# The first tile's maxima and subtractions head by head, and the matrix of one from a count by GpSimd

## The chip, the cores and the metric

The kernel runs on one core of one Trainium2 chip. The metric is the device time of one execution in microseconds: 1178.03 us is the median of 3 runs of the kernel before (1176.53 to 1178.63). The engines are named as in the profile: PE (TensorE), DVE (VectorE), ACT (ScalarE), POOL (GpSimd) and SP (SyncE, which here only issues DMAs).

## The reference

Block-causal attention, whose output goes straight through a gated feed-forward layer. Inputs: q, k, v of 8 batches x 8 heads x 576 positions x 64; weights 512 x 1536 (two) and 1536 x 512.

```python
scores = q @ k.transpose(0, 1, 3, 2) / sqrt(64)
scores = where(pos_i // 64 >= pos_j // 64, scores, -1e9)   # blocks of 64
scores = scores - scores.max(-1)
attn = exp(scores); attn = attn / (attn.sum(-1) + 1e-9)
x = (attn @ v).transpose(0, 2, 1, 3).reshape(4608, 512)
g = x @ w_gate
out = (g / (1 + exp(-g)) * (x @ w_val)) @ w_out
```

## The kernel before

The 4608 rows of x are cut into 18 tiles of 256. Attention works on pairs of heads. Scores stand transposed, keys on the 128 partitions and queries along a row, so that the maximum over keys is taken first over chunks of 128 keys (DVE) and then over the partitions (POOL, a partition all-reduce, L709). The feed-forward of a tile starts when the four head pairs of its rows are done; the first tile needs only queries and keys 0 to 255 of batch 0, and that piece of attention runs first of all.

In the code the function `attention` lists this work as tasks, each with an engine, a cost, a rank and the tasks it waits for. A planner (`in_order`) plays the costs through and writes one list of tasks per engine; the program runs those lists as they stand. Each engine is in order, so an instruction that waits holds all behind it. SP's and ACT's lists also hold the DMA issues: a DMA that waits for a landing or a semaphore holds the later ones of its queue.

For the first tile (`whole` in the code, `stays` set) the scores of a head pair are not copied out of PSUM. One PSUM buffer (`at` or `po`) has two banks, one for each head; a bank holds 384 scores per partition: 256 queries against keys 0 to 127 (chunk 0) and queries 128 to 255 against keys 128 to 255 (chunk 1). For a head pair the steps are:

- SP and ACT load q and k (L387), PE turns them with the help of the matrix of one `ident` (L411), ACT copies them out (L419), PE multiplies (L437).
- ACT hides, in place, the first 64 queries of each chunk from the upper 64 keys (L479), both heads and both chunks in one instruction; ACT copies chunk 0's queries 128 to 255 of both heads to `mx` (L482).
- DVE copies chunk 0's queries 0 to 127 of both heads to `mx` (L702) and takes the maximum of `mx` and chunk 1 (L705).
- POOL reduces `mx` over the partitions, one instruction per head (L709).
- DVE subtracts `mx` from both chunks, both heads at a time, from PSUM into `sc` (L733); ACT takes exp (L737); PE multiplies with v and with ones (L777); DVE divides (L804 to L811).

Before all that, at the program's start, DVE fills `ident`: a memset and seven doublings give the column number (L308, L311), a transposition and three additions the row number (L312, L315), and a comparison the matrix (L316). POOL at the same time zeroes two buffers for v (L260), two for `ob` (L281) and two tails of `parts` (L234). The first load of v (L754) is the third DMA of SP's list and waits for the first of these memsets.

Of the kernel before, what the change touches and what calls it, by code (L numbers as in the profile page):

```python
# [9 lines left out]
I32 = mybir.dt.int32  # L10
# [8 lines left out]
def kernel(  # L19
# [96 lines left out]
    def tiles_of(tag, place, variant=""):  # L116
        pool, variants = kinds[tag]
        slot = slots[tag][place]
        if slot[0] != variant:
            shapes, init = variants[variant]  # L120
            names = [f"{tag}{place}_{k}" for k in range(len(shapes))]
            slot[:] = variant, [
                x and pool.tile(*x, name=name, tag=name, bufs=1) for x, name in zip(shapes, names)
            ]
            if init:
                init(*slot[1])
        return slot[1]
# [36 lines left out]
    def act_us(n, psum=False, more=0.0):  # L164
        return (0.05 if psum else 0.093) + n * 0.000833 + more

    def dve_us(n, one=False):
        return 0.07 + n * (0.00052 if one else 0.00104)
# [128 lines left out]
    pool_of(psum, "gv", 2, [([P, 2 * XT], F32)])  # L297
    pool_of(psum, "po", 1, [([P, 2, DM], F32)])

    first_of = [("v", ""), ("ob", "signs" if wide else "out"), ("parts", "pair"), ("xhl", ""), ("wo", "raw"), ("hhl", "")]  # L300
    for tag, variant in first_of:
        for place in range(len(slots[tag])):
            tiles_of(tag, place, variant)


    scratch = tiles_of("t", 0)[0]
    count, mine = scratch[:, 0:P], scratch[:, P : P + 32]
    nc.vector.memset(count[:, 0:1], 0.0)  # L308
    for i in range(7):
        n = 2**i  # L310
        nc.vector.tensor_scalar(count[:, n : 2 * n], count[:, 0:n], float(n), None, ALU.add)  # L311
    nc.vector.transpose(mine, count[:, 0:32])  # L312
    for i in range(1, P // 32):
        rows = slice(32 * i, 32 * (i + 1))
        nc.vector.tensor_scalar(mine[rows, 0:1], mine[rows, 0:1], 32.0 * i, None, ALU.add)  # L315
    nc.vector.tensor_scalar(ident, count, mine[:, 0:1], None, ALU.is_equal)  # L316

    x_d = dram.tile([DM, NT], F32, name="x_d")
    s_d = dram.tile([H, NT], F32, name="s_d")
# [22 lines left out]
    def attention(R, b, h, a, e, early, bufs, lane):  # L342
# [31 lines left out]
        def piece(c, lo=0):  # L374
            return sc[0][:, :, place[c] + lo : place[c] + e - first[c]]


        def plain_scores():
# [49 lines left out]
            for visit in visits:  # L428
# [19 lines left out]
                for parts, ps in zip(visit, both):  # L448
# [25 lines left out]
                    if whole:  # L474
                        stays.append(ps)

                        def hide_there(ps=ps):
                            x = ps[0].rearrange("p x (n w) -> p x n w", w=2 * P)[:, :, :, 0:BLK]
                            nc.scalar.activation(x, x, AF.Identity, bias=unseen)  # L479

                        def max_there(ps=ps):
                            nc.scalar.copy(mx[0][:, :, L + P : L + W], ps[0][:, :, P:W])  # L482

                        t = add("ACT", act_us(4 * BLK) + 0.1, Q, hide_there, [pr], [ps])
                        t = add("ACT", act_us(2 * W), Q, max_there, [t], [ps, mx])
                        evac[0].append(t)
                        evac[1].append(t)
                        continue
# [208 lines left out]
            return stays[0][0][:, :, o + lo : o + e - first[c]]  # L697

        def merged(c, into, op, of=piece):
            if stays and op == ALU.max:  # L700

                nc.vector.tensor_copy(into[0][:, :, L : L + P], of(0)[:, :, 0:P])  # L702
            into = into[0][:, :, L + first[c] - a : L + W]
            prev = of(0, first[1] - a) if c == 1 and not stays else into
            nc.vector.tensor_tensor(into, prev, of(c), op)  # L705

        def max_all(x):
            m = mx[0][:, x, L : L + W]
            nc.gpsimd.partition_all_reduce(m, m, channels=P, reduce_op=bass_isa.ReduceOp.max)  # L709

        later = [c for run in runs for c in run if c > 1]
        ms = []
        for c in (1, *later):
            ms.append(
                add(
                    "DVE",
                    dve_us(2 * (e - first[c])),
                    Q,
                    lambda c=c: merged(c, mx, ALU.max, scores_of),
                    [*evac[0], *evac[c], *ms[0:1], *ms[-1:]],  # L720
                    [*stays, sc, mx],
                    not stays,
                )
            )
# [3 lines left out]
        exps, taken = {}, []  # L728
        for run in runs:

            def minus(c):
                m = mx[0][:, :, L + first[c] - a : L + W]
                nc.vector.tensor_tensor(piece(c), scores_of(c), m, ALU.subtract)  # L733

            def exponent(run=run):
                x = sc[0][:, :, place[run[0]] : place[run[-1]] + e - first[run[-1]]]
                nc.scalar.activation(x, x, AF.Exp)  # L737

            subs = [
                add("DVE", dve_us(2 * (e - first[c])), R, lambda c=c: minus(c), mm, [*stays, sc, mx], not stays)  # L740
                for c in run
            ]
            t = add("ACT", act_us(2 * sum(e - first[c] for c in run)), R, exponent, subs, [sc])
            exps.update({c: t for c in run})
            taken += subs
# [668 lines left out]
```

## Time and profile before

| what | value |
|---|---|
| median of 3 runs | 1178.03 us (1176.53 to 1178.63) |
| profiled execution: time, span | 1175.4 us, 1173.6 us |
| mean granted TensorE clock | 0.996 |
| PE busy | 1145.5 us, 98% of the span |
| DVE, ACT, POOL busy | 758.9, 620.4, 325.5 us |
| DMA moved | 197.40 MB, mean 168 GB/s |

A busy share is a mean over stages with different limits. In the 40 slices of the page (29.3 us each) PE shows 5, 8, 8 and then 9 to the end but for the last slice, which shows 8: PE stands idle in the first 88 us almost alone, and the changed lines all lie in the first 31 us. The views of that stretch are what matters here.

### The profile page before, as it was taken

Reading aid. Unit: us, or ns where it says so; the run is one execution under the profiler, and the core shown is the slowest. Engines: PE = TensorE matmul, PEld = TensorE weight load, DVE = VectorE, ACT = ScalarE, POOL = GpSimd, SP = SyncE. Lnnn points to the kernel's source line nnn. Section 1 sums busy time; section 2 is a strip of 40 time slices with the busy share of each in tenths; the row PEclk is TensorE's granted clock in tenths of the full one; section 3 lists DMA queues with packets and bytes.
Section 4 is the critical chain, followed back from the end, with each engine's and each line's share of the span. In section 5 each row is a group of like instructions: output and inputs, shape, how many; then the busy total and the mean of one; then the engine's idle time right before and its main releaser. Section 6 shows DMA issues by size and latency. Waiting matters only on the chain.

```text
span 1173.6 us, 21780 instructions
## 1 busy us (share of the span) xinstructions
PE 1145.5 (98%) x8512; PEld 1024.7 (87%) x8512; DVE 758.9 (65%) x1230; ACT 620.4 (53%) x1114; POOL 325.5 (28%) x139
## 2 busy tenths in 40 slices
PE   5889999999999999999999999999999999999998
PEld 4568778898898989988998899898989899999997
DVE  6988988575887668768575859575767533323222
ACT  6978876546573837465656555555646312212111
POOL 3222100144535251434444334252432500000000
PEclk9989999999999999999999999999999999999999
DMA  8658756766564756656565565655663445444432
GB/s 225 188 151 219 201 187 226 206 178 166 169 148 137 198 164 167 195 166 168 152 188 160 152 177 163 187 146 161 164 202 108 145 148 197 140 167 136 143 134 100
DMA packets 266982, 197.40 MB, mean 168 GB/s; under 512 B 195264, under 2 KB 231376, under 8 KB 266880
## 3 DMA queue, kind: packets, MB, share of 16 engines
q1 hardware_dynamic: 264304, 195.29, 56.9%
q8 instruction: 67, 1.10, 0.4%
q10 hardware_dynamic: 2576, 0.72, 0.3%
q14 instruction: 35, 0.29, 0.1%
HBM read 171.57 MB, written 24.38 MB: 167 GB/s over the span
## 4 chain that ended last, share of the span: by engine, by line
PE 85%; DVE 5%; ACT 4%; DMA 3%; issue 1%; POOL 1%; SPq 1%; ACTq 0%; DVEq 0%; POOLq 0%
PE gv L1100 16%; PE gv L1102 15%; PE gv L1101 15%; PE po L1191 7%; PE po L1193 7%; PE po L1192 7%; PE at L777 7%; PE at L564 6%; DVE sc L733 1%; DVE mx L705 1%; DMA wo<-in_moe_w_val_dram 1%; POOL mx L709 1%; DMA wo<-in_moe_w_out_dram 1%; ACT ob L959 1%; PE at L648 1%
## 5 line engine op out<-in xcount | busy, mean ns | idle before, releaser
L709 POOL PARTITION_ALL_REDUCE mx<-mx x80 | 144.1, 1850 | 408.7 <-issue 135.2
L1100 PE MATMUL gv<-xhl,v_all 128*128 128x256 f32 x864 | 241.8, 280 | 0.8 <-DVE t L1136 0.7
L1102 PE MATMUL gv<-xhl,v_all 128*128 128x256 f32 x864 | 239.7, 277 | 0.0
L1101 PE MATMUL gv<-xhl,v_all 128*128 128x256 f32 x864 | 239.3, 277 | 0.0
L828 POOL PARTITION_ALL_REDUCE mx<-mx x48 | 178.9, 3775 | 201.4 <-DVE mx L705 192.8
L1136 DVE SCALAR_TENSOR_TENSOR t<-t,gv 128x512 f32<-128x512 f32 x108 | 74.0, 685 | 215.4 <-ACT t L1133 215.2
L1100 PEld LDWEIGHTS gv<-xhl,v_all 128*128 128x128 f32 x864 | 162.1, 188 | 4.9 <-issue 2.5
L1101 PEld LDWEIGHTS gv<-xhl,v_all 128*128 128x128 f32 x864 | 162.3, 188 | 0.6
L1102 PEld LDWEIGHTS gv<-xhl,v_all 128*128 128x128 f32 x864 | 162.2, 188 | 0.2
L1133 ACT ACTIVATE t<-gv 128x512 f32<-128x512 f32 x108 | 64.6, 598 | 171.2 <-PE gv L1102 171.1
L1191 PE MATMUL po<-wo,hhl 128*128 128x512 f32 x372 | 147.7, 397 | 0.0
L1192 PE MATMUL po<-wo,hhl 128*128 128x512 f32 x372 | 145.6, 391 | 0.0
L1193 PE MATMUL po<-wo,hhl 128*128 128x512 f32 x372 | 145.1, 390 | 0.2 <-DVE hhl L1149 0.2
L1146 ACT CAST hhl<-t 128x512 fp32r<-128x512 f32 x108 | 67.0, 620 | 132.1 <-DVE t L1141 129.7
L733 DVE TENSOR_TENSOR sc<-sc,mx 128x640 f32<-128x640 f32 (+6 forms) x168 | 122.7, 765 | 11.7 <-POOL mx L709 11.6
L737 ACT ACTIVATE sc<-sc 128x1024 f32<-128x1024 f32 (+3 forms) x104 | 106.0, 1029 | 45.3 <-DVE sc L733 44.9
L1100 PE MATMUL gv<-xhl,g_even 128*128 128x256 f32 x432 | 123.7, 286 | 0.0
L1102 PE MATMUL gv<-xhl,g_even 128*128 128x256 f32 x432 | 122.2, 283 | 0.4 <-DVE g_even L981 0.4
L1101 PE MATMUL gv<-xhl,g_even 128*128 128x256 f32 x432 | 122.1, 283 | 0.0
L1100 PE MATMUL gv<-xhl,g_odd 128*128 128x256 f32 x432 | 120.7, 279 | 0.0
L1101 PE MATMUL gv<-xhl,g_odd 128*128 128x256 f32 x432 | 119.6, 277 | 0.0
L1102 PE MATMUL gv<-xhl,g_odd 128*128 128x256 f32 x432 | 119.6, 277 | 0.0
(171 smaller groups left out, 2368.8 us busy)
## 6 DMA issues: line engine op xcount, KB each, us to landing
wo<-wo_d SPq DMA_DIRECT2D x200, 512.0 KB
out_dram<-ob SPq DMA_DIRECT2D x35, 256.0 KB
v<-in_v_dram SPq DMA_DIRECT2D x64, 128.0 KB
xt<-x_d SPq DMA_DIRECT2D x64, 128.0 KB
rt<-r_d SPq DMA_DIRECT2D x128, 64.0 KB
qk<-in_q_dram SPq DMA_DIRECT2D x112, 72.0 KB
qk<-in_k_dram SPq DMA_DIRECT2D x104, 72.0 KB
x_d<-xu SPq DMA_DIRECT2D x24, 288.0 KB
```

The costliest lines, as they stand in the source:

```text
L709: nc.gpsimd.partition_all_reduce(m, m, channels=P, reduce_op=bass_isa.ReduceOp.max)
L733: nc.vector.tensor_tensor(piece(c), scores_of(c), m, ALU.subtract)
L737: nc.scalar.activation(x, x, AF.Exp)
L777: nc.tensor.matmul(ps[0][own(x), 1 - i if sums else i, q0 - s0 : s1 - s0], lhsT=ones if sums else vt[0][:, 2 * lane + c, own(x)], rhs=sc[0 ...
L828: nc.gpsimd.partition_all_reduce(m, m, channels=P, reduce_op=bass_isa.ReduceOp.add)
L1100: nc.tensor.matmul(o, lhsT=hi[:, d], rhs=xhi[:, 0:w], start=first, stop=False)
L1101: nc.tensor.matmul(o, lhsT=hi[:, d], rhs=xlo[:, 0:w], start=False, stop=False)
L1102: nc.tensor.matmul(o, lhsT=lo[:, d], rhs=xhi[:, 0:w], start=False, stop=last)
L1136: nc.vector.scalar_tensor_tensor(t[0][:, 0:n], t[0][:, 0:n], 1.0, pg[0][:, 0:n], ALU.add, ALU.mult)
L1191: nc.tensor.matmul(po, lhsT=hi, rhs=whi, start=i + y == 0, stop=False)
L1192: nc.tensor.matmul(po, lhsT=hi, rhs=wlo, start=False, stop=False)
L1193: nc.tensor.matmul(po, lhsT=lo, rhs=whi, start=False, stop=i + y == NFC - 1)
```

## The change

At the start, `ident` is made from one GpSimd count (iota: column minus row, as whole numbers) and one DVE comparison with zero. These lines now stand ahead of the loop that creates the buffers with their memsets. In the first tile, ACT's copy to `mx` is gone; ACT hides a head at a time in two instructions; DVE copies the whole of chunk 0 of a head and takes the maximum with chunk 1 of that head, then the same for the other head; the subtractions go in the order head 0 chunk 0, head 0 chunk 1, head 1 chunk 0, head 1 chunk 1. The planner's costs and the tasks stay as they were.

```diff
+    scratch = tiles_of("t", 0)[0].bitcast(I32)[:, 0:P]
+    nc.gpsimd.iota(scratch, [[1, P]], channel_multiplier=-1)
+    nc.vector.tensor_scalar(ident, scratch, 0, None, ALU.is_equal)
+
     first_of = [("v", ""), ("ob", "signs" if wide else "out"), ("parts", "pair"), ("xhl", ""), ("wo", "raw"), ("hhl", "")]
     for tag, variant in first_of:
         for place in range(len(slots[tag])):
             tiles_of(tag, place, variant)
-
-    scratch = tiles_of("t", 0)[0]
-    count, mine = scratch[:, 0:P], scratch[:, P : P + 32]
-    nc.vector.memset(count[:, 0:1], 0.0)
-    for i in range(7):
-        n = 2**i
-        nc.vector.tensor_scalar(count[:, n : 2 * n], count[:, 0:n], float(n), None, ALU.add)
-    nc.vector.transpose(mine, count[:, 0:32])
-    for i in range(1, P // 32):
-        rows = slice(32 * i, 32 * (i + 1))
-        nc.vector.tensor_scalar(mine[rows, 0:1], mine[rows, 0:1], 32.0 * i, None, ALU.add)
-    nc.vector.tensor_scalar(ident, count, mine[:, 0:1], None, ALU.is_equal)
...
-                        def hide_there(ps=ps):
-                            x = ps[0].rearrange("p x (n w) -> p x n w", w=2 * P)[:, :, :, 0:BLK]
+                        def hide_there(x, ps=ps):
+                            x = ps[0][:, x].rearrange("p (n w) -> p n w", w=2 * P)[:, :, 0:BLK]
                             nc.scalar.activation(x, x, AF.Identity, bias=unseen)
-                        def max_there(ps=ps):
-                            nc.scalar.copy(mx[0][:, :, L + P : L + W], ps[0][:, :, P:W])
-                        t = add("ACT", act_us(4 * BLK) + 0.1, Q, hide_there, [pr], [ps])
-                        t = add("ACT", act_us(2 * W), Q, max_there, [t], [ps, mx])
+                        t = add("ACT", act_us(4 * BLK) + 0.1, Q, lambda: hide_there(0), [pr], [ps])
+                        t = add("ACT", act_us(2 * W), Q, lambda: hide_there(1), [t], [ps, mx])
...
         def merged(c, into, op, of=piece):
-            if stays and op == ALU.max:
-                nc.vector.tensor_copy(into[0][:, :, L : L + P], of(0)[:, :, 0:P])
             into = into[0][:, :, L + first[c] - a : L + W]
-            prev = of(0, first[1] - a) if c == 1 and not stays else into
+            prev = of(0, first[1] - a) if c == 1 else into
             nc.vector.tensor_tensor(into, prev, of(c), op)
...
+        def max_there():
+            for x in range(2):
+                m = mx[0][:, x, L : L + W]
+                nc.vector.tensor_copy(m, scores_of(0)[:, x])
+                nc.vector.tensor_tensor(m[:, P:W], m[:, P:W], scores_of(1)[:, x], ALU.max)
...
-                    lambda c=c: merged(c, mx, ALU.max, scores_of),
+                    max_there if stays else lambda c=c: merged(c, mx, ALU.max, scores_of),
...
-            def minus(c):
-                m = mx[0][:, :, L + first[c] - a : L + W]
-                nc.vector.tensor_tensor(piece(c), scores_of(c), m, ALU.subtract)
+            def minus(c, heads=slice(0, 2)):
+                m = mx[0][:, heads, L + first[c] - a : L + W]
+                nc.vector.tensor_tensor(piece(c)[:, heads], scores_of(c)[:, heads], m, ALU.subtract)
+            def minus_there(x):
+                for c in range(2):
+                    minus(c, x)
...
-                add("DVE", dve_us(2 * (e - first[c])), R, lambda c=c: minus(c), mm, [*stays, sc, mx], not stays)
+                add("DVE", dve_us(2 * (e - first[c])), R, lambda c=c: minus_there(c) if stays else minus(c), mm, [*stays, sc, mx], not stays)
```

The order of the instructions is the same on PE and on SP, and on ACT but for the replaced ones. It moves at the program's start on POOL. POOL's list before, from the first memset to the reduction of the first head pair (`v`, `ob` and `parts` are the zeroed buffers; an ISA row without operands stands in the trace as MODIFY_POOL_CONFIG, one with `mx` as PARTITION_ALL_REDUCE):

```order
L260 MEMSET v_0_78 128x640
L260 MEMSET v_0_80 128x640
L281 MEMSET ob_0_82 128x512
L281 MEMSET ob_0_84 128x512
L234 MEMSET parts_1_87 128x64
L234 MEMSET parts_1_90 128x64
L709 ISA
L709 ISA mx_0_181<-mx_0_181 128x256 [waits DVE_49]
L709 ISA mx_0_181<-mx_0_181 128x256
```

The same piece of POOL's list in the changed kernel, whose lines are numbered anew (L302 is the count, L695 the reduction):

```order
L302 ISA
L302 IOTA t_0_78 128x128
L260 MEMSET v_0_81 128x640
L260 MEMSET v_0_83 128x640
L281 MEMSET ob_0_85 128x512
L281 MEMSET ob_0_87 128x512
L234 MEMSET parts_1_90 128x64
L234 MEMSET parts_1_93 128x64
L695 ISA
L695 ISA mx_0_174<-mx_0_174 128x256 [waits DVE_49] x4
```

The count and one more row of the kind that stands as MODIFY_POOL_CONFIG are ahead of all memsets; the row of that kind ahead of the first reduction is still there; each head's reduction now has its own wait for DVE.

DVE's list before, from the last step of `ident` through the first head pair (`at` is the PSUM buffer, `mx` the maxima, `sc` the scores):

```order
L316 TENSOR_SCALAR ident<-t_0_117 128x128 [waits DVE_49]
L702 COPY mx_0_181<-at_0_171 128x2x128 [waits PE_49,Activation_49]
L705 TENSOR_TENSOR mx_0_181<-mx_0_181,at_0_171 128x2x128
L733 TENSOR_TENSOR sc_0_218<-at_0_171,mx_0_181 128x2x256 [waits DVE_49,Pool_49]
L733 TENSOR_TENSOR sc_0_218<-at_0_171,mx_0_181 128x2x128
```

The same piece in the changed kernel:

```order
L303 TENSOR_SCALAR ident<-t_0_78 128x128 [waits Pool_49]
L701 COPY mx_0_174<-at_0_160 128x256 [waits PE_49,Activation_49]
L702 TENSOR_TENSOR mx_0_174<-mx_0_174,at_0_160 128x128 [waits DVE_49]
L701 COPY mx_0_174<-at_0_160 128x256
L702 TENSOR_TENSOR mx_0_174<-mx_0_174,at_0_160 128x128 [waits DVE_49]
L726 TENSOR_TENSOR sc_0_209<-at_0_160,mx_0_174 128x256 [waits Pool_49]
L726 TENSOR_TENSOR sc_0_209<-at_0_160,mx_0_174 128x128
L726 TENSOR_TENSOR sc_0_209<-at_0_160,mx_0_174 128x256 [waits Pool_49]
L726 TENSOR_TENSOR sc_0_209<-at_0_160,mx_0_174 128x128
```

`ident` now waits for POOL; four instructions became eight; each maximum waits for the copy just ahead of it; only the first copy waits for ACT, so it waits for both heads' hiding.

SP's first DMAs are in the same order before and after (here from the kernel before): the loads of v stand between the first and the later loads of q, and wait for POOL.

```order
L387 DMA qk_0_137<-in_q_dram 96x3x64 x2
L754 DMA v_0_78<-in_v_dram 128x2x64 [waits Pool_49]
L754 DMA v_0_78<-in_v_dram 128x2x64
L387 DMA qk_0_145<-in_q_dram 96x3x64 [waits DMAHW1_49]
L387 DMA qk_0_145<-in_q_dram 96x3x64 [waits DMAHW3_49]
L387 DMA qk_0_145<-in_q_dram 96x3x64 [waits DMAHW5_49]
L387 DMA qk_0_145<-in_q_dram 96x3x64 [waits DMAHW7_49]
L387 DMA qk_0_137<-in_q_dram 96x3x64 [waits DMAHW0_49]
L387 DMA qk_0_137<-in_q_dram 96x3x64 [waits DMAHW1_49]
L944 DMA wo_0_108<-in_moe_w_gate_dram 128x4x256 [waits DMAHW2_49]
```

No row moved here; what POOL's memset now stands behind is new.

## The prediction

> **What bounds the kernel now.** I read the page's slices first, then the busy times by stretch, then the chain of waits and the timeline of the first 20 us, because the changed lines run there only. The page, its span and PE's 40 slices of 29.3 us:
>
> ```profile
> span 1173.6 us, 21780 instructions
> PE   5889999999999999999999999999999999999998
> ```
>
> After three slices PE is full to the end, with a fixed list of work. Time lost or won in the start therefore comes out at the end, unless something in the start absorbs it. Busy times in the first stretches (per engine in the header's order: PE, PE's weight load, DVE, ACT, POOL; then clock, DMA share, GB/s):
>
> ```profile
> 0.00:10.00 10.00, 4.07 (x21) 3.05 (x21) 3.93 (x19) 3.45 (x7) 2.96 (x11) 1.00 0.77 178
> 10.00:20.00 10.00, 7.68 (x54) 6.09 (x54) 5.82 (x14) 8.68 (x18) 5.90 (x6) 1.00 0.95 244
> 20.00:30.00 10.00, 6.00 (x51) 4.15 (x51) 9.69 (x21) 7.70 (x15) 2.48 (x2) 1.00 0.86 244
> 30.00:40.00 10.00, 7.32 (x71) 5.18 (x67) 9.55 (x22) 9.40 (x18) 2.76 (x2) 1.00 0.66 162
> ```
>
> In the first 10 us nobody but the DMAs is busy: it is a stage of loads and waits. From 20 us DVE is the bound (9.69 and 9.55 of 10). The chain of waits of the first 30 us (start, length, what) says how the first stage hangs together:
>
> ```profile
> 5.93 0.31 SPq L387
> 6.29 2.36 DMA qk<-in_q_dram
> 8.78 1.19 PE gv L411 x6
> ...
> 14.57 0.31 ACT mx L482
> ...
> 15.75 2.12 POOL mx L709 x2
> ...
> 17.90 0.40 DVE sc L733
> ...
> 27.17 2.49 POOL mx L709 x2
> ```
>
> The second head pair's q, the last of eight q loads in SP's queue, sets when PE goes on (8.78), and all that follows: its hiding, its maxima, POOL's reduction, DVE's subtraction. So whatever holds SP's queue in the first 6 us is on the path. The timeline of the start (start, length, engine, line):
>
> ```profile
> 0.73 1.20 POOL L260 MEMSET v<- 128x640 f32 x2 [0.29 <-POOLq L1397]
> ...
> 1.09 0.06 DVE L308 MEMSET t<- 128x1 f32 x1
> ...
> 1.69 0.97 SPq L754 DMA_DIRECT2D v<-in_v_dram  x2
> 1.73 1.28 ACT L1244 ACT_TABLE_LOAD   x1 [1.73 <-PEq L1397]
> ...
> 1.87 1.04 POOL L281 MEMSET ob<- 128x512 f32 x2
> 2.85 0.23 POOL L234 MEMSET parts<- 128x64 f32 x2
> 2.98 3.77 SPq L387 DMA_DIRECT2D qk<-in_q_dram  x6
> ...
> 3.15 2.17 ACTq L387 DMA_DIRECT2D qk<-in_k_dram  x4
> ...
> 4.10 0.28 DVE L316 TENSOR_SCALAR ident<-t 128x128 f32<-128x128 f32 x1
> ...
> 4.44 1.22 PE L411 MATMUL gv<-ident,qk 96*128 96x96 f32 x6 [4.44 <-DVE ident L316]
> 5.37 0.74 ACT L419 ACTIVATE parts<-gv 128x288 f32<-128x288 f32 x2 [2.15 <-DMA qk<-in_k_dram]
> ...
> 7.86 0.45 ACT L479 ACTIVATE at<-at,unseen 128x256 f32<-128x256 f32 x1 [1.75 <-PE at L437]
> 8.34 0.37 ACT L482 COPY mx<-at 128x256 f32<-128x256 f32 x1
> 8.74 0.42 DVE L702 COPY mx<-at 128x256 f32<-128x256 f32 x1 [4.36 <-ACT mx L482]
> ...
> 9.09 0.41 DVE L705 TENSOR_TENSOR mx<-mx,at 128x256 f32<-128x256 f32 x1
> ...
> 9.59 2.11 POOL L709 PARTITION_ALL_REDUCE mx<-mx  x2 [6.51 <-DVE mx L705]
> ...
> 11.73 1.02 DVE L733 TENSOR_TENSOR sc<-at,mx 128x512 f32<-128x512 f32 x2 [2.24 <-POOL mx L709]
> ...
> 12.67 0.68 DVE L968 SCALAR_TENSOR_TENSOR wo<-wo,ob 128x512 int32<-128x512 int32 x1
> ...
> 13.90 0.69 DVE L973 SCALAR_TENSOR_TENSOR wo<-wo 128x512 int32<-128x512 int32 x1 [0.55 <-ACT wo L963]
> ...
> 14.91 0.42 DVE L702 COPY mx<-at 128x256 f32<-128x256 f32 x1 [0.31 <-ACT mx L482]
> ...
> 17.90 1.02 DVE L733 TENSOR_TENSOR sc<-at,mx 128x512 f32<-128x512 f32 x2 [1.24 <-POOL mx L709]
> ```
>
> SP's third DMA, the load of v at 1.69, waits for POOL's first memset, and six loads of q (2.98) are queued behind it. POOL is idle for 6.51 us ahead of its first reduction.
>
> **The change part by part.** *The count.* It takes 3.3 us of DVE work away (1.09 to 4.38, DVE idle otherwise) and puts two instructions ahead of POOL's memsets: the count, and the ISA row ahead of it. Such a row stands ahead of the first reduction already; line L709's own instructions show it:
>
> ```profile
> L709 POOLq MODIFY_POOL_CONFIG  x2: 7/7/7, 3.1 to 3.1; - x2
> ```
>
> It is a change of POOL's code, 7 ns as recorded; what it really takes is hidden. It started at 3.1 and the first reduction at 9.59, 0.09 after DVE's end at 9.50, so it took 6.4 us or less. That is the upper bound by rows. The only load of an engine's tables that has a duration is ACT_TABLE_LOAD, 1.28 us: my lower bound. The gap belongs to the same instruction on the same engine, so I go near it: 6.0 us. The count itself: the nearest POOL row over 128x128 is a memset, and the v memset (1.20 for two, about 0.63 each) bounds it above;
>
> ```profile
> L241 POOL MEMSET qk<- 128x128 f32 x1 | 0.3, 276 | 0.0
> ```
>
> I take 0.4 (0.28 to 0.63).
>
> [...]
>
> *What stands behind it.* The first v memset ended at about 1.36; now at 0.73 + 6.0 + 0.4 + 0.63 = 7.76, and SP issues v at about 7.85 in place of 1.69: 6.2 later. SP's waits in the first 9 us were:
>
> ```profile
> SPq L387 <- DMA qk<-in_k_dram: 0.8, 1, 0.8
> SPq L387 <- DMA v<-in_v_dram: 0.5, 1, 0.5
> SPq L387 <- DMA qk<-in_q_dram: 0.3, 1, 0.3
> ```
>
> From v's issue to PE's start on the second pair it was 8.78 - 1.69 = 7.1 us. The wait for k (0.8) falls away, since ACT's queue, which POOL doesn't hold, has brought k by then; the others stay. So 6.3 to 7.1 are left: PE starts at 14.1 to 14.9, 5.4 to 6.2 later. I take 5.6. SP's next DMAs, the first weights and the next q and k, move along.
>
> `ident` itself would be there at 0.73 + 6.4 + 0.1 + 0.28 = 7.5 in place of 4.38, 3.1 later: the first pair's, and less than the above.
>
> *The second change of code* now starts after the memsets, which took 0.73 to 3.08: at 7.13 + 2.35 = 9.5, and ends at 15.5. The first reduction moves from 9.59 to 15.6, the subtraction that ended at 12.75 to 18.5 (5.8 later). DVE's work between it and the second pair's maxima, two weight operations (12.67 and 13.90), is some 1.3 us; the maxima could start at 19.8, against 14.91 + 5.6 = 20.5 from the loads. So the second change has 0.7 us to spare; each microsecond more per change costs the path by the loads one and this one two.
>
> *Heads apart.* DVE, per head pair: a copy and a maximum of 256 each took 9.50 - 8.74 = 0.76, overlapped by 0.07. Now a copy of 256 (0.42) and a maximum of 128 (0.28, as the 128x128 row at 4.10) that waits for it, per head: 0.72 + 0.65 = 1.37, 0.6 more. Subtractions: 0.42 and 0.28 per head, overlapped, 1.2 against 1.02: 0.2 more. ACT: its copy (0.37) goes, the hiding (0.45) becomes two; a hiding of 128x128 took 0.36 to 0.41 at other places:
>
> ```profile
> 29.12 0.36 ACT L469 ACTIVATE sc<-po,unseen 128x128 f32<-128x128 f32 x1
> ```
>
> so 0.75 to 0.85 against 0.85: nothing gained, since DVE's first copy waits for both. POOL starts head 0 after 0.72 in place of 0.76: nothing. Head 0's subtractions can start one reduction (1.05) earlier, which hides the longer subtractions where DVE waits for POOL (1.24 at 17.90). Left on DVE once it is the bound: the fourth pair's maxima 0.6 and 0.2 each for three pairs, 1.2, less what its waits for POOL swallow. I take 0.6 (0 to 1.2).
>
> *Sum.* 5.6 + 0.6 = 6.2 us. The profiled execution took 1175.4 (span 1173.6 and 1.8 around it), so its like would be 1181.6; the median of the runs shown lies 2.6 above it, at 1178.03, so 1184.2.
>
> **The rivals.** *Cheap change of code* (chance 0.21, 1179.3). At 1.28 us the v memset ends at 3.04, SP is 1.4 late and wins 0.8 back; with DVE's 0.6 that is 1.2. The same result if later waits swallow most of the delay. For it: nothing in the trace has a visible load on POOL. Against: nothing bounds it below 6.4 either, and PE's list, SP's queue and DVE all hang on the same late loads.
>
> *Faster* (chance 0.07, 1175.4). The chain runs through whole reductions of two heads (2.12 at 15.75, and one of 2.49 at 27.17). With heads apart DVE can start after the first, 1.05 earlier at each place, and ACT's copy (0.31 at 14.57) leaves the chain: up to 2.6 off. It decides only if a change of code costs under about 1.3 us, so that SP isn't held, and if DVE isn't full when head 0 arrives; at 20 to 30 us it has 0.31 us free.
>
> *Much slower* (chance 0.14, 1189). Two changes of code in a row at 8 us each, while the loads run: the second ends at 0.73 + 8.4 + 2.35 + 8 = 19.5, the first subtractions at 22.4, the second pair's maxima at 23.7 in place of 14.91, 8.8 later, and with the 0.6 that is 9.4; with a full 1.2 on DVE and the next reductions bunched behind the late ones (2.12 a pair) it is up to 12, so some 11. It decides from 6.7 us per change. Against it: the one in the trace took no more than 6.4 with DMAs busy at 0.77.
>
> **How the numbers follow.** Forecast 0.58, rivals 0.21, 0.07, 0.14. About 0.2% (2.4 us) is what a measurement of this kernel can tell from no change. The forecast's own range: 4.5 to 6.4 us per change of code, 0.6 more for SP if it wins nothing back, and 0 to 1.2 for DVE, so 4.1 to 7.8 late, 1182.1 to 1185.8. With most of the cheap case and the nearer part of the much slower one it is 1178.8 to 1189.5. Faster 0.07, same 0.20 (most of the cheap case), slower 0.73.
>
> **What would show it.** In the changed kernel's timeline: POOL's count near 7 and its v memsets after it; SP's load of v near 7.8; the second pair's turning on PE near 14.4; the first reduction near 15.6 with POOL's idle time ahead of it released by no one; ACT's copy gone; DVE's maxima at 1.37 per pair. From there every place in the first 70 us should be about 6 later, with DMA nearly idle before 8. It is wrong if v is issued before 4, or if the delay shrinks between 20 and 70 us because a wait there was longer than the chain shows.

## The result, and the profile after

| | before | changed |
|---|---|---|
| median (lowest to highest), us | 1178.33 (1176.53 to 1179.15) | 1184.51 (1183.24 to 1185.66) |
| profiled execution: time, span, us | 1175.4, 1173.6 | 1184.42, 1182.6 |

The medians lie 6.2 us apart, and the 1184.51 us stand against a forecast of 1184.2 (the kernel before has one execution more here than in its first table, 1179.15). The ratio on record, 1.0064 with a 95% interval of 1.0052 to 1.0076, is not the quotient of these medians, which is 1.0052. Of 1178.33 us its interval is 6.1 to 9.0 us, so 6.2 lies at its lower edge. The two profiled executions lie 9.0 us apart, at its upper edge; the last paragraphs of this section say what is known of that.

The page of the changed kernel, its span and PE's 40 slices:

```profile
span 1182.6 us, 21784 instructions
PE   4789999999999999999999999999999999999998
```

PE is full after three slices, as before (5, 8, 8 and then nines); the first two are one tenth emptier, and the span is longer by what the start lost. The timeline of the changed kernel's start (start us, length us, engine, line; in brackets the engine's idle time ahead and what ended it):

```profile
7.96 0.23 POOL L302 IOTA t<- 128x128 int32 x1 [7.52 <-issue]
8.16 1.19 POOL L260 MEMSET v<- 128x640 f32 x2
8.23 2.31 DVE L303 TENSOR_SCALAR ident<-t 128x128 f32<-128x128 int32 x1 [7.09 <-POOL t L302]
8.80 0.91 SPq L751 DMA_DIRECT2D v<-in_v_dram  x2
...
10.23 0.23 POOL L234 MEMSET parts<- 128x64 f32 x2
...
14.49 2.44 PE L403 MATMUL gv<-ident,qk 96*128 96x96 f32 x12 [0.53 <-DMA qk<-in_q_dram]
14.76 0.42 DVE L701 COPY mx<-at 128x256 f32<-128x256 f32 x1 [4.22 <-ACT at L471]
15.22 0.29 DVE L702 TENSOR_TENSOR mx<-mx,at 128x128 f32<-128x128 f32 x1
...
15.88 0.29 DVE L702 TENSOR_TENSOR mx<-mx,at 128x128 f32<-128x128 f32 x1
...
16.59 2.15 POOL L695 PARTITION_ALL_REDUCE mx<-mx  x2 [6.14 <-DVE mx L702]
...
18.77 0.62 DVE L726 TENSOR_TENSOR sc<-at,mx 128x256 f32<-128x256 f32 x2 [0.45 <-POOL mx L695]
...
19.32 0.68 DVE L965 SCALAR_TENSOR_TENSOR wo<-wo,ob 128x512 int32<-128x512 int32 x1
...
19.85 0.33 ACT L471 ACTIVATE at<-at,unseen 128x128 f32<-128x128 f32 x1
...
20.10 0.69 DVE L970 SCALAR_TENSOR_TENSOR wo<-wo 128x512 int32<-128x512 int32 x1
...
20.71 0.42 DVE L701 COPY mx<-at 128x256 f32<-128x256 f32 x1
```

POOL does nothing for 7.5 us and then counts. Its two gaps begin at the ISA rows of the changed kernel's lines L302 and L695 (durations in ns; behind them the first and last start):

```profile
L302 POOLq MODIFY_POOL_CONFIG  x2: 11/11/11, 0.8 to 0.8; - x2
L695 POOLq MODIFY_POOL_CONFIG  x2: 5/5/5, 10.7 to 10.7; - x2
```

From 0.8 to the count at 7.96 are 7.1 us; from 10.7 to the first reduction at 16.59 are 5.9. The row at 16.59 names DVE's maximum as the releaser, but head 0's maximum had ended at 15.22 + 0.29 = 15.51, 1.1 us earlier: DVE did not hold it. That these waits go with the rows is what the experiments bear out: with late reductions alone the same gap, 6.19 us, has no releaser. What a row of this kind does is in no trace; "a change of code" is the author's name for the time from such a row to the instruction behind it. SP's waits in the first 16 us of the changed kernel:

```profile
SPq L751 <- POOL v L260: 7.2, 1, 7.2
SPq L379 <- DMA v<-in_v_dram: 0.2, 1, 0.2
```

The load of v is issued at 8.80 in place of 1.69, 7.1 later. The waits of 0.8, 0.5 and 0.3 us behind it have shrunk to one of 0.2, so 1.4 us are won back, and PE turns the second pair at 14.49 in place of 8.78: 5.7 later. From there the whole start is late. The busy times of the changed kernel by stretch (columns as in the prediction):

```profile
0.00:10.00 10.00, 0.00 (x0) 0.00 (x0) 2.00 (x5) 1.49 (x2) 2.24 (x9) 1.00 0.34 76
10.00:20.00 10.00, 8.36 (x48) 6.60 (x49) 3.72 (x10) 5.17 (x13) 2.60 (x5) 1.00 0.80 190
20.00:30.00 10.00, 5.87 (x47) 4.33 (x46) 9.66 (x27) 7.91 (x16) 4.20 (x4) 0.80 0.93 258
```

In the first 10 us PE now has no matmul at all (4.07 busy before) and the DMAs move 76 GB/s in place of 178. At 20 to 30 us DVE is busy for 9.66 of 10 us (9.69 before), which leaves it little room to catch up.

PE runs the same instructions in the same order in both kernels, so each matmul of the one can be set against the same matmul of the other. The lag, worked out that way from the two traces:

| at (us of the kernel before) | 4.4 | 8.8 | 15.0 | 17.4 | 21.1 | 23.6 | 27.2 | 33 to 37 | 45 to 51 | 55 to 63 | 85 | 197 | 301 to the end |
|---|---|---|---|---|---|---|---|---|---|---|---|---|---|
| changed kernel is late by (us) | 6.2 | 5.7 | 5.1 | 5.3 | 7.0 | 8.6 | 7.2 | 6.6 | 8.3 | 7.6 | 7.7 | 8.8 | 9.0 |

Some 6 us are lost before the first score is subtracted, and they are never given back. The lag then goes up and down between 6.5 and 8.6 us and is 7.7 at 85 us. In parts of these stretches the granted clock (third column from the right above) was below 1: in this execution 0.80 at 20 to 30 us, 0.86 at 30 to 40, 0.84 at 50 to 60 and 0.69 at 70 to 80, while the profiled execution of the kernel before had such stretches only here:

```profile
60.00:70.00 10.00, 6.69 (x43) 3.94 (x43) 9.82 (x20) 8.47 (x18) 1.50 (x2) 0.80 0.39 94
70.00:80.00 10.00, 10.00 (x84) 7.82 (x81) 7.38 (x16) 5.00 (x12) 2.47 (x2) 0.86 0.58 171
```

Read in windows of 2 us the granted clock there goes down to 0.50: at 66 to 72 us in the kernel before (0.52, 0.50, 0.50), and at 26 to 32, 50 to 52 and 74 to 80 in the changed kernel. The mean granted clock was 0.993 in this profiled execution and 0.996 in that of the kernel before; in the executions of the kernels below it was 0.987 to 0.997, with no tie to whether the kernel was slower (0.991 to 0.996 for the count alone, 0.991 to 0.995 for the heads alone). The last 1.3 us, from 7.7 to 9.0, come between 118 and 301 us, where the granted clock was 1.00 in both, so the clock does not account for them. How much of the 2.8 us by which the profiled pair lies further apart than the medians belongs to the change is not shown; its size is 6.2 us by the medians and 6.1 to 9.0 by the interval.

### The profile page after: what moved, and what is told of

Read it like the earlier page. It is cut to its first block, busy times and chain, and to the rows that moved or that the text cites. A ratio compares the mean times of both kernels' runs of the same rounds, so it can differ in the third digit from the quotient of the medians.

```text
span 1182.6 us, 21784 instructions
## 1 busy us (share of the span) xinstructions
PE 1149.2 (97%) x8512; PEld 1026.9 (87%) x8512; DVE 761.4 (64%) x1234; ACT 620.6 (52%) x1114; POOL 324.8 (27%) x140
## 4 chain that ended last, share of the span: by engine, by line
PE 85%; ACT 5%; DVE 4%; DMA 3%; issue 2%; SPq 1%; POOL 0%; DVEq 0%; POOLq 0%; ACTq 0%
PE gv L1097 16%; PE gv L1099 15%; PE gv L1098 15%; PE po L1188 7%; PE po L1190 7%; PE po L1189 7%; PE at L774 7%; PE at L553 6%; ACT sc L734 1%; DMA wo<-in_moe_w_gate_dram 1%; ACT ob L956 1%; DMA wo<-in_moe_w_out_dram 1%; DMA wo<-in_moe_w_val_dram 1%; PE po L774 1%; PE at L637 1%
## 5 line engine op out<-in xcount | busy, mean ns | idle before, releaser
L695 POOL PARTITION_ALL_REDUCE mx<-mx x80 | 143.2, 1839 | 412.7 <-issue 135.1
```

## The experiments

The theory on record: GpSimd's count forces two changes of POOL's code; the first holds SP's queue and so the loads of q, and it alone sets the delay (5.6 us), the second being hidden by 0.7 us; the heads cost 0.6. Rivals: the loss comes from the heads; or it comes from the late first reduction, by way of DVE; or a change of code costs little and something else holds the start.

### The heads alone

The changed kernel with `ident` made on DVE as before:

```diff
-    scratch = tiles_of("t", 0)[0].bitcast(I32)[:, 0:P]
-    nc.gpsimd.iota(scratch, [[1, P]], channel_multiplier=-1)
-    nc.vector.tensor_scalar(ident, scratch, 0, None, ALU.is_equal)
...
+    scratch = tiles_of("t", 0)[0]
+    count, mine = scratch[:, 0:P], scratch[:, P : P + 32]
+    nc.vector.memset(count[:, 0:1], 0.0)
...
+    nc.vector.tensor_scalar(ident, count, mine[:, 0:1], None, ALU.is_equal)
```

> The kernel before with the heads-apart edits alone (hiding, maxima, subtractions); the matrix of one is made by DVE as before, so POOL has one change of code, after its memsets. Theory of the prediction (the code change ahead of the v memset carries 5.6 us, the heads 0.6): 1178.3 + 0.6 = about 1179, within 0 to 1.2 of the kernel before; the second head pair turned on PE at 8.8, first reduction at 9.6. Rival 'heads': DVE's eight instructions in place of four carry the loss, then 3 us or more over before (1181.5 or above). Rival 'gain given back': the heads apart win time (subtractions of head 0 start a reduction earlier), then 1 us or more under before.

Measured: 1177.38 us against 1176.23, ratio 1.0008 (0.9995 to 1.0022). Its timeline:

```profile
10.81 0.62 DVE L734 TENSOR_TENSOR sc<-at,mx 128x256 f32<-128x256 f32 x2 [0.54 <-POOL mx L703]
...
15.13 0.42 DVE L709 COPY mx<-at 128x256 f32<-128x256 f32 x1 [0.27 <-PE gv L411]
...
17.75 1.14 DVE L734 TENSOR_TENSOR sc<-at,mx 128x256 f32<-128x256 f32 x4
```

DVE does start on head 0 after one reduction, at 10.81 in place of 11.73, but there it has time to spare. The second pair's maxima start at 15.13 (14.91 before) and its subtractions at 17.75 (17.90 before), four in a row with no wait for POOL: the wait of 1.24 us that was there is filled with the longer maxima. The edit pays with one hand what it wins with the other, and the time shows neither (the interval is 0.6 us under to 2.6 over). The heads are not where 6 us went.

### The count alone

The kernel before with the count edit, and nothing of the heads:

```diff
+    scratch = tiles_of("t", 0)[0].bitcast(I32)[:, 0:P]
+    nc.gpsimd.iota(scratch, [[1, P]], channel_multiplier=-1)
+    nc.vector.tensor_scalar(ident, scratch, 0, None, ALU.is_equal)
...
-    nc.vector.memset(count[:, 0:1], 0.0)
...
-    nc.vector.tensor_scalar(ident, count, mine[:, 0:1], None, ALU.is_equal)
```

> The kernel before with the count edit alone: GpSimd's count and its change of code ahead of the memsets; maxima and subtractions as before. Theory of the prediction: 5.6 us over before, about 1184, most of the whole change; v issued by SP at about 8.8, the second pair turned at about 14.5, the comparison for the matrix of one again about 2.3 us long beside the memsets. Rival 'heads': under 3 us over before.

Measured: 1182.92 us against 1176.23, ratio 1.0052 (1.0033 to 1.0070). Its timeline:

```profile
7.97 0.23 POOL L301 IOTA t<- 128x128 int32 x1 [7.53 <-issue]
...
8.81 0.91 SPq L746 DMA_DIRECT2D v<-in_v_dram  x2
...
16.36 2.15 POOL L701 PARTITION_ALL_REDUCE mx<-mx  x2 [5.89 <-DVE mx L697]
```

All of the loss is here, with the same two gaps on POOL as in the changed kernel. This run has both waits, SP's and the late reduction's, so it does not say which of them counts.

### Late reductions alone

The kernel before, with a count whose result nobody uses, behind POOL's memsets. The loads then keep their time, and the first reduction stands behind a count, as in the changed kernel:

```diff
     nc.vector.tensor_scalar(ident, count, mine[:, 0:1], None, ALU.is_equal)
 
+    nc.gpsimd.iota(tiles_of("t", 1)[0].bitcast(I32)[:, 0:P], [[1, P]], channel_multiplier=-1)
+
```

> The kernel before plus a count that nobody uses, placed after POOL's memsets and ahead of the first reduction: two changes of code in a row, but SP's load of v isn't held and the matrix of one comes from DVE as before. It tells the hold of SP's queue from the lateness of the reductions. Theory 'SP's queue' (the prediction's sum): 0 to 1 us over before, since the loads are on time. Rival 'late reductions': first reduction at about 3.1 + 7.1 + 0.3 + 5.9 = 16.4 in place of 9.6, DVE's subtraction and the second pair's maxima behind it at about 20 to 20.5 in place of 14.9, so 5 us over before.

Measured: 1182.90 us against 1176.23, ratio 1.0053 (1.0036 to 1.0071): as slow as the count edit, with every load in its old place. Its timeline:

```profile
1.69 0.97 SPq L756 DMA_DIRECT2D v<-in_v_dram  x2
...
8.82 2.43 PE L413 MATMUL gv<-ident,qk 96*128 96x96 f32 x12 [0.76 <-DMA qk<-in_q_dram]
...
10.36 0.23 POOL L318 IOTA t<- 128x128 int32 x1 [7.29 <-issue]
...
16.78 2.15 POOL L711 PARTITION_ALL_REDUCE mx<-mx  x2 [6.19 <-issue]
...
18.96 1.02 DVE L735 TENSOR_TENSOR sc<-at,mx 128x512 f32<-128x512 f32 x2 [9.22 <-POOL mx L711]
...
21.30 0.42 DVE L704 COPY mx<-at 128x256 f32<-128x256 f32 x1
```

The second pair is turned at 8.82 as ever, but DVE sits for 9.22 us at the first subtraction, and the second pair's maxima, behind it in DVE's list, start at 21.30 in place of 14.91. So the late reductions, with nothing else late, lose all of it. The expectation's 0 to 1 us asked more of the prediction's sum than it says: there the second change was hidden behind SP's hold by 0.7 us, and by itself put these maxima at 19.8, 4.9 late. Whether it was hidden must be read from the changed kernel.

### SP's hold alone

To hold SP without delaying the reductions, a memset and a reduction of unused columns were put ahead of the memsets in the kernel before. The first MODIFY_POOL_CONFIG row then stands ahead of v's memset, and none is left ahead of the real reductions:

```diff
-    first_of = [("v", ""), ("ob", "signs" if wide else "out"), ("parts", "pair"), ("xhl", ""), ("wo", "raw"), ("hhl", "")]
...
+    with tc.manual_schedule():
+        early = tiles_of("t", 1)[0][:, 0:64]
+        nc.gpsimd.memset(early, 1.0)
+        nc.gpsimd.partition_all_reduce(early, early, channels=P, reduce_op=bass_isa.ReduceOp.max)
+        first_of = [("v", ""), ("ob", "signs" if wide else "out"), ("parts", "pair"), ("xhl", ""), ("wo", "raw"), ("hhl", "")]
...
```

> The kernel before plus a reduction of 64 columns of scratch that nobody uses, ahead of all POOL memsets: one change of code in all, at the front, so that SP's load of v is held until about 0.8 + 6 to 7 + 0.7 + 0.6 = 8 to 9, while the first real reduction waits for no change of code. Theory 'SP's queue': 5 to 6 us over before. Rival 'late reductions': 0 to 1 us over before. If both this kernel and the one with the late reduction lose about 5 us, either wait is enough alone and the two lie side by side.

Measured: 1176.91 us against 1176.23, ratio 1.0002 (0.9991 to 1.0014). The run missed its purpose and showed something else. The ISA row of its early reduction:

```profile
L303 POOLq MODIFY_POOL_CONFIG  x2: 11/11/11, 0.9 to 0.9; - x2
```

and its timeline:

```profile
1.01 0.52 POOL L303 PARTITION_ALL_REDUCE t<-t  x1
...
2.14 0.91 SPq L757 DMA_DIRECT2D v<-in_v_dram  x2
```

The reduction started 0.1 us behind its row (0.9 to 1.01): SP was never held. The kernel before ends its POOL work with reductions, so a guess was that the cost depends on what POOL ran last, in the execution ahead too, and that only a kernel with a count in between pays. The next run adds just that: an unused count of one element at the very end of POOL's list.

```diff
             t.fn()
+        nc.gpsimd.iota(unseen.bitcast(I32), [[1, 1]], channel_multiplier=1)
```

> The kernel with the unused reduction at the front, plus an unused count at the very end of POOL's list (after its last reduction), so that the next execution starts with the count's code in POOL and not the reduction's. One theory formed from the runs so far: a change of code costs about 6 to 7 us when the other code is there and nothing when it is there already, and an execution starts with what the last one left. It expects the front reduction to start near 7 to 8 in place of 1.0, v issued by SP at about 8 to 9, and, as the first real reduction then waits for no change of code, the hold of SP's queue alone: second pair turned on PE at about 14, 5 to 6 us over before. Rival: a change of code from this kind of line is cheap wherever it stands ahead of a small reduction; then as without the count at the end, within 1 us of before.

Measured: 1182.08 us against 1177.07, ratio 1.0045 (1.0033 to 1.0058). The same ISA row and the timeline:

```profile
L303 POOLq MODIFY_POOL_CONFIG  x2: 11/11/11, 1.1 to 1.1; - x2
```

```profile
7.31 0.54 POOL L303 PARTITION_ALL_REDUCE t<-t  x1 [6.44 <-issue]
...
10.02 2.20 POOL L712 PARTITION_ALL_REDUCE mx<-mx  x2
...
14.32 2.43 PE L414 MATMUL gv<-ident,qk 96*128 96x96 f32 x12 [6.57 <-DMA qk<-in_q_dram]
...
20.44 0.42 DVE L705 COPY mx<-at 128x256 f32<-128x256 f32 x1 [0.31 <-ACT mx L485]
```

One instruction at the end of the program has turned 0.1 us at its start into 6.2 (1.1 to 7.31), as the guess said. The added count itself ran at 951.04 us, 229 us before the end, with no work of POOL behind it. Two things stay open. That the count stood at the end, and not only that the program had one, is not tried apart. And no run has a count that follows a count with no reduction in between: in six traces POOL waited 7.1 to 8.2 us ahead of a count each time (the 8.2 is POOL's idle time ahead of the added count here). The reductions started 5.7 to 6.2 us behind their row where a count had come in between (six traces), and 0.1 us behind it with no count in the program (one trace).

This is now the test that was meant: the first reduction is at 10.02, near its 9.59, and only SP is held. The second pair is turned at 14.32, its maxima start at 20.44, and the kernel is 5.0 us slower. So each of the two waits alone makes nearly all of the loss. They lie side by side, and the later one counts.

### One wait taken out of the changed kernel

If so, freeing SP in the changed kernel wins little. Here the v buffers are zeroed by DVE, which is idle then:

```diff
-    pool_of(const, "v", 2, [([P, NKC, 2 * D], F32)], lambda t: nc.gpsimd.memset(t, 0.0))
+    pool_of(const, "v", 2, [([P, NKC, 2 * D], F32)], lambda t: nc.vector.memset(t, 0.0))
```

> The changed kernel with the two v buffers zeroed by DVE in place of POOL: SP's load of v isn't held, all else as in the changed kernel; POOL has 1.2 us less ahead of its second change of code. Theory 'either wait is enough': the first reduction still starts at 15.4 to 15.6 (16.6 in the changed kernel), so 1 us under the changed kernel, about 5 over before. Theory 'SP's queue' (the prediction's sum): the loads are on time and most of the loss is gone, 1 to 2 us over before.

Measured: 1181.07 us against 1177.07, ratio 1.0038 (1.0026 to 1.0050). Its timeline:

```profile
1.84 0.94 SPq L751 DMA_DIRECT2D v<-in_v_dram  x2
...
8.34 1.16 DVE L303 TENSOR_SCALAR ident<-t 128x128 f32<-128x128 int32 x1 [5.85 <-POOL t L302]
...
12.86 2.46 PE L403 MATMUL gv<-ident,qk 96*128 96x96 f32 x12
...
15.49 2.15 POOL L695 PARTITION_ALL_REDUCE mx<-mx  x2 [6.08 <-DVE mx L702]
...
19.61 0.42 DVE L701 COPY mx<-at 128x256 f32<-128x256 f32 x1
```

v is issued at 1.84 again, yet 4.0 us of the loss stay. The second pair's maxima start 1.10 us earlier than in the changed kernel (19.61, not 20.71), which is just what the first reduction won (15.49, not 16.59), with two memsets fewer ahead of it on POOL. In the changed kernel it is the late reduction that comes last: ACT had the second pair's scores ready at 19.85 + 0.33 = 20.18, and DVE turned to them at 20.71.

The run also shows a third wait. PE turns the second pair at 12.86 without waiting for a load, but not at 8.78, since the first pair stands ahead of it and waits for `ident`, which the count makes late (9.50 in place of 4.38). So this run frees SP but not the whole path by way of PE.

### The count behind the memsets

The kernel before, with `ident` from the count, but behind POOL's memsets, so that SP is free and the late reduction and a late `ident` are left:

```diff
-    nc.vector.memset(count[:, 0:1], 0.0)
...
-    nc.vector.tensor_scalar(ident, count, mine[:, 0:1], None, ALU.is_equal)
+    scratch = tiles_of("t", 0)[0].bitcast(I32)[:, 0:P]
+    nc.gpsimd.iota(scratch, [[1, P]], channel_multiplier=-1)
+    nc.vector.tensor_scalar(ident, scratch, 0, None, ALU.is_equal)
```

> The kernel before with the matrix of one from GpSimd's count, but the count placed after POOL's memsets. It shows whether the 2.3 us of DVE's comparison in the changed kernel came from POOL's memsets beside it: then the comparison, with no memset beside it, takes about 0.3 us here. If the whole numbers are what is slow, it takes 2.3 here too. First product on PE near 10.8, first reduction near 16.8, about 6 to 7 us over before.

A single time, so without an interval: 1184.43 us, against 1177.07 for the kernel before. Its timeline:

```profile
10.48 0.23 POOL L307 IOTA t<- 128x128 int32 x1 [7.44 <-issue]
10.74 0.23 DVE L308 TENSOR_SCALAR ident<-t 128x128 f32<-128x128 int32 x1 [9.61 <-POOL t L307]
```

Neither place that was tried for the count helps: the 7.4 us ahead of it are paid here too. The comparison took 0.23 us here, where no memset of POOL runs beside it, against 2.31 in the changed kernel, where it ended at 10.54, just behind the last memset (10.46), and 1.16 with two memsets fewer, where it ended at 9.50.

### Three other orders of the start

If the second pair's q behind v sets the path, then loading v later should win something. In the kernel before, the first load of v was moved behind the first tile's last load of q:

```diff
     order = in_order()
+    sp = [t for t in order if t.engine == "SP"]
+    order.remove(sp[1])
+    order.insert(order.index(sp[4]) + 1, sp[1])
```

> The kernel before with one thing moved in SP's list: the first two loads of v stand behind all loads of q of the first tile, with the planner's order of everything else as it was. If the last q load sets the first stage, as the chain says, the second pair is turned about 1 us earlier than at 8.8 (two issues, 0.97, and the wait for v's landing, 0.5, are gone from ahead of it), and the kernel is up to 1 us under before. Rival: ACT's and DVE's own work takes the room, then no difference.

Measured: 1175.69 us against 1177.07, ratio 0.9989 (0.9980 to 0.9998). Its timeline:

```profile
8.21 2.56 PE L411 MATMUL gv<-ident,qk 96*128 96x96 f32 x12
```

The second pair is turned 0.6 us earlier (8.78 before). It is the one version with a lower time than the kernel before, by 1.4 us, less than the 0.2% named in the prediction. A later wait of ACT, for weights, will matter for the next run:

```profile
22.91 0.78 ACT L959 ACTIVATE ob<-wo 128x512 f16<-128x512 f32 x1 [1.70 <-DMA wo<-in_moe_w_out_dram]
```

Then all first loads were put in the order of the pairs, on both queues:

```diff
     order = in_order()
+    for engine, turn in (("SP", (0, 4, 2, 3, 1)), ("ACT", (0, 3, 1, 2))):
+        loads = [t for t in order if t.engine == engine and t.moves][: len(turn)]
+        places = [order.index(t) for t in loads]
+        for p, n in zip(places, turn):
+            order[p] = loads[n]
```

> The kernel before with the first loads put in the order in which PE uses them: on SP q of the first pair, q of the second, then q of the third and fourth, then v; on ACT k in the same order of pairs. All else as in the kernel before. If the last load of the second pair holds the first stage, as the chain of before says (5.93 to 8.64), the second pair is turned at about 7 in place of 8.8, the first stage ends earlier, and the kernel is 1 to 2 us under before (v behind all q alone gave 1.4 under). Rival: from 8 us on ACT's copies and DVE's maxima set the pace and take the gain back; then no difference.

Measured: 1177.30 us against 1176.35, ratio 1.0006 (0.9995 to 1.0017). Its timeline:

```profile
8.15 2.56 PE L411 MATMUL gv<-ident,qk 96*128 96x96 f32 x12
...
22.66 0.79 ACT L959 ACTIVATE ob<-wo 128x512 f16<-128x512 f32 x1 [1.50 <-DMA wo<-in_moe_w_out_dram]
```

And the row of the kernel before that answers to the second:

```profile
21.79 0.80 ACT L959 ACTIVATE ob<-wo 128x512 f16<-128x512 f32 x1 [0.20 <-DMA wo<-in_moe_w_out_dram]
```

The second pair is 0.6 us earlier here too, and ACT then waits 1.50 us in place of 0.20 for weights, which may be what takes the gain back. It is not shown: with v alone behind q ACT waited 1.70 us, the second pair's maxima started at 14.53 (14.48 here), and yet that time was lower. So it is open why the one order came out 1.4 us under and the other not, and neither gain nor loss of these orders can be relied on.

Last, the heads edits on top of that order, where DVE gets its first pairs earlier (`hide_there`, `max_there` and `minus_there` as in the change):

```diff
-                        t = add("ACT", act_us(2 * W), Q, max_there, [t], [ps, mx])
+                        t = add("ACT", act_us(2 * W), Q, lambda: hide_there(1), [t], [ps, mx])
...
-                    lambda c=c: merged(c, mx, ALU.max, scores_of),
+                    max_there if stays else lambda c=c: merged(c, mx, ALU.max, scores_of),
...
```

> The same order of the first loads together with the heads-apart edits (hiding, maxima, subtractions). It tells whether head by head pays once the loads are earlier. If DVE's eight instructions in place of four are hidden by its waits for the reductions: as the order of loads alone, within 1 us. If DVE is the bound there, 0.5 to 2 us more than the order of loads alone.

Measured: 1177.60 us against 1176.35, ratio 1.0009 (0.9999 to 1.0019). The second pair's maxima start at 13.88, 1.0 us before their old place, and the heads neither pay nor cost anything that can be told here either.

### One row for all

The start of the second pair's maxima (DVE's first copy from the second pair's PSUM, each from the timeline of its run) against the time:

| kernel | second pair's maxima start, us (before: 14.91) | first reduction, us | time against the kernel before, us | ratio (95%) |
|---|---|---|---|---|
| heads alone | 15.13 | 9.71 | +1.2 | 1.0008 (0.9995 to 1.0022) |
| early reduction, no count | 15.36 | 10.88 | +0.7 | 1.0002 (0.9991 to 1.0014) |
| v after q | 14.53 | 10.05 | -1.4 | 0.9989 (0.9980 to 0.9998) |
| loads in the order of the pairs | 14.48 | 10.00 | +1.0 | 1.0006 (0.9995 to 1.0017) |
| the same with the heads | 13.88 | 9.59 | +1.3 | 1.0009 (0.9999 to 1.0019) |
| changed, v zeroed by DVE | 19.61 | 15.49 | +4.0 | 1.0038 (1.0026 to 1.0050) |
| SP's hold alone | 20.44 | 10.02 | +5.0 | 1.0045 (1.0033 to 1.0058) |
| changed kernel | 20.71 | 16.59 | +6.2 | 1.0064 (1.0052 to 1.0076) |
| count alone | 20.87 | 16.36 | +6.7 | 1.0052 (1.0033 to 1.0070) |
| late reductions alone | 21.30 | 16.78 | +6.7 | 1.0053 (1.0036 to 1.0071) |
| count behind the memsets | 21.34 | 16.82 | +7.4 | a single time |

The times are differences of medians, the ratios those on record; they need not agree to the tenth. Where that copy starts 4.7 to 6.4 us late, the kernel ends 4 to 7 us late, whichever wait made it late. Among the slower ones most intervals overlap; only the changed kernel and the one with v zeroed by DVE just part (1.0052 and 1.0050). What is shown is the step between the first five and the others. Where the copy starts earlier than before, nothing clear is won.

## Why the prediction was right, point by point

- *Sign and size:* 1184.2 forecast, 1184.51 measured. The cause named, two waits on POOL that hold up the start, is the one (7.1 and 5.9 us; the count alone 1.0052, the heads alone 1.0008). That they are changes of code was the author's reading and is not shown. That the number fits to 0.3 us is in good part luck: the change is 6.1 to 9.0 us by its interval, and of the sum's two terms the wait behind the 5.6 was not the one that came last, and the 0.6 cannot be told from nothing.
- *A change of code, 6.0 us:* the first, ahead of the count, took 7.1, over the upper bound of 6.4; the second, ahead of the reduction, 5.9. One price was put on two kinds of instruction. The value was about right, but the reason for it wasn't: "it took 6.4 us or less" was read from the gap of the kernel before between 3.1 and 9.59, which DVE ended. The early reduction's run, which ends with the same reductions, took 0.1 us at such a row, so that the gap very likely held no such wait and bounds none. So the cheap change of code, the first rival, seems to describe the kernel before rightly; it fell because the changed kernel runs a count and reductions in turn.
- *The count, 0.4 us:* 0.23, below the lower bound of 0.28.
- *v issued at 7.85, PE on the second pair at 14.4:* 8.80 and 14.49. Two misses cancel: the wait ahead of the count took 1.1 longer, and SP won back 1.4 us where 0 to 0.8 was allowed, because the waits for v and q shrank too and not the one for k alone.
- *`ident` at 7.5 by a comparison of 0.28 us:* it took 2.31 and ended at 10.54. The step priced it by a row that had no POOL memset beside it. By way of POOL it costs nothing: head 0's maximum, at 15.51, still came 1.1 us before the reduction could start. But it was 6.2 late and not 3.1, and PE, which waited only 0.53 for q at 14.49, could not have turned the second pair before 13.96. The prediction set this wait aside as the smaller one; it stood 0.5 us behind SP's.
- *"So the second change has 0.7 us to spare":* this is the step that failed. The first reduction came at 16.59 (15.6 forecast), the subtractions ended at 18.77 + 0.62 = 19.39 (18.5), and from there to the second pair's maxima at 20.71 (19.8) DVE worked without a break. The path by the loads was ready at 20.18 (20.5). So the second change did not have 0.7 us to spare but came 0.5 too late: the first change's 1.1 us more went whole into this path, while on the other SP won more back. Late reductions alone lose 6.7 us, SP's hold alone 5.0, and with SP free the changed kernel still loses 4.0. The sum put on one wait what several waits side by side each hold, and it came out because they are worth nearly the same.
- *The heads, 0.6 us (0 to 1.2):* 0.08% (-0.05 to 0.22), some 1 us that cannot be told from nothing. DVE's maxima took 15.88 + 0.29 - 14.76 = 1.41 a pair where 1.37 was worked out. The rival that called them a gain of up to 2.6 us falls: DVE does start one reduction earlier, where it has time to spare.
- *Much slower (1189):* it needed two changes of code of 8 us. They were 7.1 and 5.9; the first is over the 6.7 from which it was to decide, but the second is not. A single wait of over 8 us did occur, ahead of the count that one run has at its end (8.2).
- *"About 6 later in the first 70 us":* 5.1 to 8.6 in the profiled pair, and it did not shrink. The DMAs were less idle before 8 us than written: a share of 0.41 (0.73 before). From 20 us on that execution has lost more than the medians did, 9.0 in the end, partly beside low clocks at places of its own, partly at full clock; why is left open.

## What to carry to other kernels

Before an instruction is given to GpSimd, look at which POOL instructions stand behind a MODIFY_POOL_CONFIG row, which of them the program ends with, and what is queued behind POOL at that place: here one count of 0.23 us brought two waits, of 7.1 and 5.9 us, into the start. When an edit delays several things that meet again later, price each alone; a slack of 0.7 us between estimates of 6 is no slack, and taking one of them away leaves most of the loss (here 4.0 of 6.2 us). And a cost that is hidden in the profile has no upper bound from the gap that hides it unless something shows that it was paid at all (here 0.1 us in place of "6.4 us or less").

## What the runs showed of the hardware that was not expected

*The same row on POOL cost 0.1 us or 6.2.* The same MODIFY_POOL_CONFIG row ahead of the same reduction took 0.1 us where POOL's list ended with reductions, and 6.2 us where it ended with a count of one element that took 0.13 us itself. In the changed kernel, which counts first and reduces later, both waits are paid: 7.1 and 5.9 us. The wait ahead of a count took 7.1 to 8.2 us in six traces, the wait ahead of a reduction that followed a count 5.7 to 6.2. What POOL does in that time is not shown.

*A `tensor_scalar` on DVE beside POOL's memsets took longer and ended just behind one.* The comparison of 128x128 took 0.23 us with no memset beside it. In the changed kernel it took 2.31, to the end of the last of six memsets, and 1.16 where there were four. It shows in the kernel before as well, where DVE's six first doublings run beside the memsets:

```profile
1.20 2.16 DVE L311 TENSOR_SCALAR t<-t 128x1 f32<-128x1 f32 x6
```

and in the run with SP's hold alone, where they run while POOL stands idle ahead of its early reduction (for six, 0.97 us less):

```profile
1.18 1.19 DVE L314 TENSOR_SCALAR t<-t 128x1 f32<-128x1 f32 x6
```

The comparison ended 0.08 us behind the last memset with six and with four. But the second to fifth doubling of the kernel before ended 0.02 to 0.06 us behind one memset each, while the comparison lasted until all six were done, and no run here shows what decides between the two. DVE's own memsets beside POOL's first one took no more than where POOL stood still (0.06 us for 128x1 in both). What in the chip makes a `tensor_scalar` take longer beside a memset is not shown.
